# Wide first products for pairs of tiles, second products ten steps behind, some subtractions on ScalarE

## The chip, the cores and the metric

The kernel runs on one core of one Trainium2 chip. The metric is the device time of one execution in microseconds (us). Before the change it is 302.31 us, the median of three runs (301.88 to 303.08).

Five engines work side by side, each through its own queue in program order: TensorE (matmuls; PE in the profile, with weight loads listed apart as PEld), VectorE (DVE), ScalarE (ACT), GpSimd (POOL) and SyncE (SP). SP, ACT and POOL also issue DMA transfers, and an engine stands while an instruction of its queue waits.

## The reference

An attention in a sliding window, followed by a two-layer network with an ELU between. Cut to what matters:

```python
def _attn_ref(q, k, v):                      # (8, 8, 576, 64): batch, heads, sequence, head size
    scores = scale * np.matmul(q, k.transpose(0, 1, 3, 2))
    mask = np.abs(pos[:, None] - pos[None, :]) <= 32
    scores = np.where(mask, scores, -1000000000.0)
    attn = np.exp(scores - np.max(scores, axis=-1, keepdims=True))
    attn = attn / (np.sum(attn, axis=-1, keepdims=True) + 1e-09)
    return np.matmul(attn, v)

def _moe_ref(x, w_in, w_out):                # x: (4608, 512), w_in: (512, 2048), w_out: (2048, 512)
    h = x @ w_in
    g = np.where(h > 0.0, h, np.exp(np.minimum(h, 0.0)) - 1.0)
    return g @ w_out
```

## The kernel before

**The network** is done in 18 tiles of 256 tokens. A tile has 8 steps, so there are 144 steps, counted by `kk`; `order[kk]` says which tile and which part of it a step does. Step `kk` makes two groups of 128 of the 2048 hidden features. Its *products* (`mm1`, `products`, L734) are 8 matmuls: two feature groups by four parts of the 512 inputs, each 256 columns wide. They go to one bank of PSUM, `h0` or `h1` in turn. ScalarE then takes exp of the bank (`exponents`, L744), VectorE subtracts one (`subtract`, L756; in steps 1, 3 and 4 ScalarE does it, L754), and VectorE makes g = min(max(h, 0), exp(h) - 1) from the bank and that (`elu`, L767). This last operation is issued at the beginning of step `kk + 1`, and with it the bank is free for the products of step `kk + 2`. g is kept in 8 buffers.

**The sums** (`mm2`, `add`, `sums_to`, L787) multiply g by w_out: four matmuls of 512 columns a step, two for each half of the tile's tokens, added up over the tile's 8 steps in the banks `y0` and `y1`. They run two steps (`LAG`) behind the products. With a tile's last sum, ScalarE copies y0 and VectorE copies y1 out of PSUM (`rows_out`, `copy_out`), and SP stores them. From step 132 on the sums are taken from a list `todo`, three or four a step, and `last_sums` does the rest, with the very last half tile cut into 384 and 128 columns so that its last copy is small.

**The attention** works on 36 pairs of 64-row query blocks; two pairs are the 256 tokens of one tile. From pair 6 on two pairs go together and start at step `begin[i]`, 14 steps ahead of the tile's first step: scores of both at `begin` (32 small matmuls, L384), the exp of each on ScalarE at `begin` and `begin + 1` (L395), `mask` on VectorE at `begin + 1` and `begin + 2` (L404), P.V of both at the end of `begin + 2` (`pv`, 32 small matmuls, L416), `normalize` on VectorE at `begin + 3` and `begin + 4` (L425, L428), and then `x_dma` (L455): a DMA transpose on SP that puts the pair's 128 tokens into `xT`, the input of the products. `xT` has one buffer a tile, five in turn.

**Feeding the attention**, for each batch of 576 rows: q and k are loaded as fp32 on SP (`load_qk`, L132), cast in three parts each on ScalarE (`cast_qk`), written to DRAM by ScalarE's queue (`write_rows`) and read back transposed by SP (`transpose_rows`, L324). V is loaded by GpSimd's queue (`load_v`, L151). Every second query block needs V shifted by 64 rows: `rotate_v` makes that with VectorE copies (L175), `rotate_v_dma` with two DMAs on SP (L183). Batches 2 and 3 use the DMAs, batches 4 to 7 four VectorE copies each.

**What sets the order.** It is written out by hand. `at(kk, slot, ...)` notes a task for a step, and the loop at the end runs a step as: g of the step before, the tasks "dve", the products, the tasks "mid", the sums, the tasks "end". Each engine's queue holds its instructions in the order in which this loop issues them.

Of the kernel before, what the change touches and what calls it, by code (L numbers as in the profile page):

```python
# [9 lines left out]
FP32 = mybir.dt.float32  # L10
# [11 lines left out]
def kernel(  # L22
# [100 lines left out]
    def load_qk(b, which, part, engs=(nc.sync, nc.sync)):  # L123
        z, nj = part
        mj = max(nj, HJ)
        t = lpool.tile([128, 2, mj * D], FP32, tag=f"f{which}{mj}",
                       name=f"f{which}", bufs=2 if part is WHOLE else 1)
# [166 lines left out]
    def cast_qk(b, which, part, j0, n, eng, hs=slice(0, 2)):  # L294
        z, nj = part
        if (b, which, z) not in qk_b:
            qk_b[b, which, z] = lpool.tile(
                [128, max(nj, HJ), 2 * D], BF16,
                tag=f"b{which}{max(nj, HJ)}", name="qkb",
                bufs=2 if part is WHOLE else 1)  # L300
# [142 lines left out]

    def xT_of(i):
        t, z = i // 2, i % 2
        if z == 0:
            xT[t] = xpool.tile([128, 2, NDO, 128], BF16, tag="xT", name="xT")
        return xT[t][:, z, :, :]
# [173 lines left out]
    for i in range(FIRST_TWO, NPAIR):  # L622
        begin[i] = begin.get(i - i % 2, STEPS * (i // 2) - 14)
# [17 lines left out]
    at(BACK_AT, "dve", swap_back)  # L641
    starts = set(begin.values())
    starts |= {begin[i] + 1 for i in range(FIRST_TWO, NPAIR)}
    for b in range(2, B):
# [3 lines left out]
        l_qk, l_v, c0 = {2: (0, 0, 0), 3: (15, 24, 22), 4: (35, 36, 41),  # L648
# [9 lines left out]
        if b <= 3:  # L658
# [3 lines left out]
            at((21, 28)[b - 2], "mid", rotate_v_dma, b, 3 - b)  # L662
# [16 lines left out]
        for n, (which, j0) in enumerate(  # L679
                (which, j0) for which in range(2) for j0 in (0, 6, 12)):  # L680
            at(free[n], "end", cast_qk, b, which, WHOLE, j0, 6,
               nc.vector if free[n] < 26 else nc.scalar)
            if j0 == 12:
                at(free[n], "end", write_rows, b, which)
                at(free[n] + (3 if free[n] == 29 else 4), "mid",
                   transpose_rows, b, which)

    order = [(z, n + m) for n in range(0, HALF, 2) for z in range(2)  # L690
             for m in range(2)]
    order += [(z, n) for n in range(HALF, STEPS) for z in range(2)]
    order += [(t, n) for t in range(2, NT) for n in range(STEPS)]
    psH, e_t, m_t, g_t, psY = {}, {}, {}, {}, {}

    def mm1(kk):
        t, s = order[kk]
        if kk == BY_PAIRS[1]:
            return
        ks = BY_PAIRS if kk == BY_PAIRS[0] else (kk,)  # L700
        tags = ((f"h{kk % 2}", "s") if kk == NSTEP - 1 else
                ("s",) if kk == 2 else ("u",) if kk == 3 else (f"h{kk % 2}",))
# [6 lines left out]
        for p in range(len(ks)):  # L709
            for k in ks:  # L710
                for z in range(len(tags)):
                    products(k, z, p if len(ks) > 1 else None)
                if p == len(ks) - 1:
                    for z in range(len(tags)):
                        exponents(k, z)
                        if k == NSTEP - 1:
                            elu(k, z)
# [4 lines left out]
    def products(kk, z, pair):  # L722
        t, s = order[kk]
        ps = psH[kk][z]
        w = ps.shape[1]
        for j in range(w):
# [21 lines left out]

    def subtract(kk, z):
# [3 lines left out]
        if kk in (1, 3, 4):  # L753
# [5 lines left out]
    def elu(kk, z=0):  # L759
        if z == 0:  # L760
            g_t[kk] = mpool.tile([128, FG, TT], BF16, tag="g_sb", name="g_sb",
                                   bufs=8)
# [18 lines left out]
    def sums_to(n, ts, j, c=0):  # L781
        t, s = order[n]
        if (s, ts, j) == (0, 0, 0):
            tags = ("h2", "t0") if t == 1 else ("y0", "y1")
            psY[t] = [ps_tile([128, D_MODEL], FP32, g, "psY")
                      for g in tags + ("u",) * (t == NT - 1)]
        nc.tensor.matmul(  # L787
            sum_of(t, ts, c), lhsT=g_t[n][:, j, ts * 128:(ts + 1) * 128],
            rhs=w_out_sb[:, s * FG + j, cols_of(c)],
            start=(s == 0 and j == 0),  # L790
            stop=(s == STEPS - 1 and j == FG - 1))
# [13 lines left out]
    def add(n, ts, j):  # L805
        t, s = order[n]
        for c in (1, 2) if (t, ts) == (NT - 1, 1) else (0,):
            sums_to(n, ts, j, c)
        if s == STEPS - 1 and (ts, j) == (1, FG - 1):
# [3 lines left out]
    def mm2(n):  # L813
        for ts in range(2):
            for j in range(FG):
                add(n, ts, j)
# [3 lines left out]
    LAG, LATE = 2, NSTEP - 14  # L820
    todo = [(n, ts, j) for n in range(LATE, NSTEP)
            for ts in range(2) for j in range(FG)]

    def last_sums():
        rest = sorted({n for n, _, _ in todo})
        assert len(todo) == len(rest) * 2 * FG
        def some(ns, ts, c):
            for n in ns:
                for j in range(FG):
                    sums_to(n, ts, j, c)  # L830
# [58 lines left out]
```

## Time and profile before

The profile is of one execution. Its own time is 302.52 us; the span from its first to its last instruction is 300.8 us, and the granted TensorE clock in it is 0.999.

| what | value |
|---|---|
| median of three runs | 302.31 us |
| profiled execution / its span | 302.52 us / 300.8 us |
| exp of the products, L744, ScalarE, 128x512 | 143 of 599 ns |
| subtraction, L756, VectorE, 128x512 | 140 of 435 ns |
| subtraction, L754, ScalarE, 128x512 | 3 of 631 ns |
| g, L767, VectorE, 128x512 | 143 of 690 ns |
| mask, L404, VectorE | 32 of 682 ns |
| normalisation, L425 and L428, VectorE | 36 of 199 ns and 36 of 692 ns |
| copies of y, VectorE and ScalarE, 128x512 | 17 of 683 ns, 18 of 586 ns |
| V rotation, L175, VectorE | 20 of 425 ns |
| cast of a third of q or k, ScalarE | 26 of 829 ns |
| transpose of x, L455, issue to landing | 2.6 us median, 26 issues |
| load of V, L151, issue to landing | 12.6 us median |

A count and a mean come from the groups of instructions with different shapes kept apart. A group of the page reads: line, engine, operation, output and inputs with shape, count, then busy time and mean ns of one, then the idle time of the engine just before these instructions and what ended it. Matmuls overlap each other, so their durations add up to more than the time they take: their pace is read from their starts. Some matmul records are missing from the trace, which shows as a count of 7 where 8 ran.

### The profile page before, as it was taken

The page shows a single profiled execution, that of the slowest core. Times are in us where ns is not written, and L with a number is a line of the kernel's source. Part 1 is how long each engine was busy: PE and PEld are TensorE (multiplying, and loading weights), DVE is VectorE, ACT ScalarE, POOL GpSimd, SP SyncE. Part 2 cuts the span into 40 slices and gives each one's busy share as a digit, 9 for nine tenths or more (in the row PEclk, how much of TensorE's full clock was granted, in tenths as well). Part 3 has the DMA queues.
Part 4 walks back from the last instruction along what each step waited for, and adds up shares of the span by engine and source line. Part 5 has one row for each costly group of instructions (what it writes and reads, how often), then busy time and mean ns, then how long its engine had stood idle before and what let it go on. Part 6 is the DMA issues. An engine that isn't in the chain of part 4 may idle for free.

```text
span 300.8 us, 7664 instructions
## 1 busy us (share of the span) xinstructions
PE 291.8 (97%) x3066; PEld 198.6 (66%) x3118; DVE 240.9 (80%) x479; ACT 170.2 (57%) x258; POOL 52.7 (18%) x74
## 2 busy tenths in 40 slices
PE   7899999999999999999999999999999999999995
PEld 3585567677666666666666666666666666666673
DVE  7788588978787988888889789887988787877773
ACT  3783648688655567456745665467535353534342
POOL 8777203520005000410032002300000000000000
PEclk9999999999999999999999999999999999999999
DMA  9999999999957978999899989997921111111011
GB/s 190 168 200 203 185 233 349 370 179 231 241 159 199 239 116 270 244 267 135 161 256 323 172 203 252 312 153 137 268 54 72 35 72 38 70 37 70 2 70 71
DMA packets 94070, 52.68 MB, mean 175 GB/s; under 512 B 78163, under 2 KB 83795, under 8 KB 94035
## 3 DMA queue, kind: packets, MB, share of 16 engines
q1 hardware_dynamic: 47330, 35.61, 44.7%
q0 software_dynamic: 44976, 10.10, 44.2%
q10 hardware_dynamic: 1728, 6.49, 6.3%
q8 instruction: 24, 0.39, 0.6%
q14 instruction: 12, 0.09, 0.1%
HBM read 36.70 MB, written 15.34 MB: 173 GB/s over the span
## 4 chain that ended last, share of the span: by engine, by line
PE 85%; DMA 5%; issue 3%; DVE 2%; ACT 2%; POOL 2%; POOLq 0%; ACTq 0%; DVEq 0%
PE ps L734 39%; PE psY L787 38%; PE psS L416 4%; DMA out_dram<-y_sb 3%; PE psS L384 3%; DMA c<-in_k_dram 2%; ACT e_sb L744 1%; DVE g_sb L767 1%; PE ptx L335 1%; PE psXT L438 1%; POOL Vo L158 1%; DVE qkb L292 0%; ACT qkb L290 0%; PE ptx L340 0%; PE psS L364 0%
## 5 line engine op out<-in xcount | busy, mean ns | idle before, releaser
L744 ACT ACTIVATE e_sb<-ps 128x512 f32<-128x512 f32 (+1 forms) x145 | 86.3, 596 | 113.4 <-PE ps L734 106.0
L734 PE MATMUL ps<-xT,w_in_sb 128*128 128x256 bf16 (+1 forms) x1168 | 149.7, 271 | 0.1
L787 PE MATMUL psY<-w_out_sb,g_sb 128*128 128x512 bf16 (+2 forms) x541 | 139.3, 373 | 2.9 <-issue 0.3
L734 PEld LDWEIGHTS <-w_in_sb 128*128 128x128 bf16 x1168 | 110.4, 98 | 36.8 <-issue 0.8
L767 DVE SCALAR_TENSOR_TENSOR g_sb<-ps,m_sb 128x512 bf16<-128x512 f32 (+1 forms) x145 | 99.3, 686 | 13.1 <-DVE m_sb L756 0.5
L756 DVE TENSOR_SCALAR m_sb<-e_sb 128x512 bf16<-128x512 f32 (+1 forms) x142 | 61.5, 433 | 34.3 <-ACT e_sb L744 32.3
L787 PEld LDWEIGHTS <-g_sb 128*128 128x128 bf16 x592 | 55.9, 98 | 38.7
L151 POOL DMA_DIRECT2D Ve<-in_v_dram x37 | 32.5, 892 | 132.8 <-PE psS L416 79.5
L395 ACT ACTIVATE pu<-psS 128x1024 bf16<-128x1024 f32 x36 | 36.6, 1023 | 0.9 <-PE psS L384 0.8
L428 DVE TENSOR_TENSOR x_st<-psS,rc 128x512 bf16<-128x512 f32 x36 | 24.9, 692 | 1.2
L290 ACT CAST qkb<-f 128x768 bf16<-128x768 f32 (+1 forms) x29 | 25.0, 862 | 0.0
L404 DVE TENSOR_TENSOR pm<-pu,masks 128x1024 bf16<-128x1024 bf16 x32 | 21.8, 682 | 0.0
L416 PEld LDWEIGHTS <-pm 128*64 128x64 bf16 x512 | 9.6, 110 | 7.3 <-DVE pm L404 6.5
L292 DVE COPY y_sb<-psY 128x512 f32<-128x512 f32 (+1 forms) x18 | 12.2, 676 | 1.5 <-PE psY L787 1.5
L384 PEld LDWEIGHTS <-kT 64*128 64x128 bf16 x560 | 9.4, 95 | 4.6 <-issue 4.4
L290 ACT COPY y_sb<-psY 128x512 f32<-128x512 f32 (+1 forms) x19 | 10.8, 569 | 2.5 <-PE psY L787 2.5
L384 PE MATMUL psS<-qT,kT 64*128 64x64 bf16 x560 | 11.8, 191 | 0.1
L416 PE MATMUL psS<-Ve,pm 128*64 128x65 bf16 x288 | 11.5, 196 | 0.1
L290 ACT COPY qT<-ptx 128x1152 bf16<-128x1152 bf16 (+4 forms) x9 | 7.7, 882 | 5.0 <-PE ptx L340 3.5
L416 PE MATMUL psS<-Vo,pm 128*64 128x65 bf16 x224 | 10.3, 196 | 0.0
L175 DVE COPY Vo<-Ve 64x1040 bf16<-64x1040 bf16 (+1 forms) x22 | 9.1, 413 | 0.7
L425 DVE RECIPROCAL rc<-psS 128x8 f32<-128x8 f32 x36 | 7.2, 199 | 0.9 <-PE psS L416 0.9
(54 smaller groups left out, 91.3 us busy)
## 6 DMA issues: line engine op xcount, KB each, us to landing
out_dram<-y_sb SPq DMA_DIRECT2D x36, 256.0 KB, 3.5
f<-in_q_dram SPq DMA_DIRECT2D x12, 576.0 KB, 6.3
f<-in_k_dram SPq DMA_DIRECT2D x12, 576.0 KB, 8.0
in_dram<-qkb ACTq DMA_DIRECT2D x10, 576.0 KB, 4.2
Ve<-in_v_dram POOLq DMA_DIRECT2D x21, 128.0 KB, 12.6
w_out_sb<-in_moe_w_out_dram POOLq DMA_DIRECT2D x3, 512.0 KB, 10.4
Ve<-in_v_dram POOLq DMA_DIRECT2D x14, 96.0 KB, 11.6
w_in_sb<-in_moe_w_in_dram POOLq DMA_DIRECT2D x2, 512.0 KB, 10.4
```

The costliest lines, as they stand in the source:

```text
L151: nc.gpsimd.dma_start(out=V_e[b % 3][p0:p1, m, :, 0:D], in_=v[b, :, lo + p0:lo + p1, :].rearrange("h p d -> p h d"))
L290: nc.scalar.copy(d_, s_)
L384: nc.tensor.matmul(psS[:, h % 2, hp * 128 + z * QB:hp * 128 + (z + 1) * QB], lhsT=keys, rhs=qT[b % 2][base:base + 64, hp, QB * qb:QB * (qb ...
L395: nc.scalar.activation(pu, _bap(psS, [psS.ap[0], [1, 1024]]), AX.Exp, scale=SCALE)
L404: nc.vector.tensor_mul(pm, pu, _bap(mm, [mm.ap[0], [0, H], [1, 2 * QB]]))
L416: nc.tensor.matmul(psS[QB * z:QB * (z + 1), par, hp * VD:(hp + 1) * VD], lhsT=pm[:, par * HP + hp, z * QB:(z + 1) * QB], rhs=vv[:, qb // 2 ...
L428: nc.vector.tensor_mul(x_st, _bap(psS, [psS.ap[0], [VD, HP], [512, 2], [1, D]]), _bap(rc, [rc.ap[0], [2, HP], [1, 2], [0, D]]))
L734: nc.tensor.matmul(o, lhsT=w_in_sb[:, do, fo * 128:(fo + 1) * 128], rhs=r, start=(do == 0), stop=(do == NDO - 1))
L744: nc.scalar.activation(e_sb, ps, AX.Exp)
L756: nc.vector.tensor_scalar(m_sb, e_sb, -1.0, None, ALU.add)
L767: nc.vector.scalar_tensor_tensor(g_t[kk][:, z * w:(z + 1) * w, :], ps, 0.0, m_t.pop((kk, z)), ALU.max, ALU.min)
L787: nc.tensor.matmul(sum_of(t, ts, c), lhsT=g_t[n][:, j, ts * 128:(ts + 1) * 128], rhs=w_out_sb[:, s * FG + j, cols_of(c)], start=(s == 0 an ...
```

## The change

1. **Wide products.** From tile 8 on (`WIDE`), two tiles share their products. A step makes one feature group for both tiles: 4 matmuls of 512 columns, where a step made two groups for one tile with 8 matmuls of 256 columns. A pair of tiles has 16 such steps, 64 to 79 for tiles 8 and 9. `xT` becomes one buffer for the four pairs of two tiles (two in turn), and for the earlier tiles four buffers. The attention of tiles 8 to 17 begins two steps earlier.
2. **Sums from a list.** From step 18 on all sums of tiles 2 to 16 come from `todo`, in order: four a step, or three in the steps of the set `light` from step 31 (`FALL`) on, as long as fewer than 48 (`LEAD`) are owed; a tile's last sums are finished in the step when at most one more than these is left. The sums of the last tile are done after all others, in `last_sums`, in the banks h0, u and s. g has 23 buffers.
3. **Subtraction.** Besides steps 1, 3 and 4, ScalarE subtracts in steps 30 to 89 that are two to four steps after the begin of pairs 8 to 19 and have no cast: steps 30, 33, 34, 35, 39, 50, 51 and 52.
4. **Feeding.** Batch 4's V is rotated by DMAs at step 43; its casts start at step 40. The load and cast tiles of q and k are two in turn for wholes and halves alike, where halves had their own.

```diff
     def load_qk(b, which, part, engs=(nc.sync, nc.sync)):
         z, nj = part
-        mj = max(nj, HJ)
-        t = lpool.tile([128, 2, mj * D], FP32, tag=f"f{which}{mj}",
-                       name=f"f{which}", bufs=2 if part is WHOLE else 1)
+        t = lpool.tile([128, 2, SJ * D], FP32, tag=f"f{which}",
+                       name=f"f{which}")
...
     def xT_of(i):
-        t, z = i // 2, i % 2
+        n = 2 if i < 2 * WIDE else 4
+        t, z = i // n * n // 2, i % n
         if z == 0:
-            xT[t] = xpool.tile([128, 2, NDO, 128], BF16, tag="xT", name="xT")
+            xT[t] = xpool.tile([128, n, NDO, 128], BF16, tag=f"xT{n}",
+                               name="xT", bufs=4 if n == 2 else 2)
...
-        begin[i] = begin.get(i - i % 2, STEPS * (i // 2) - 14)
+        begin[i] = begin.get(i - i % 2, STEPS * (i // 2) - 14 - 2 * (i >= 2 * WIDE))
...
-        l_qk, l_v, c0 = {2: (0, 0, 0), 3: (15, 24, 22), 4: (35, 36, 41),
+        l_qk, l_v, c0 = {2: (0, 0, 0), 3: (15, 24, 22), 4: (35, 36, 40),
...
-        if b <= 3:
+        if b <= 4:
...
-            at((21, 28)[b - 2], "mid", rotate_v_dma, b, 3 - b)
+            at((21, 28, 43)[b - 2], "mid", rotate_v_dma, b, int(b == 2))
...
-    order += [(t, n) for t in range(2, NT) for n in range(STEPS)]
+    order += [(t, n) for t in range(2, WIDE) for n in range(STEPS)]
+    made = {(t, n * FG + j): (kk, j * TT)
+            for kk, (t, n) in enumerate(order) for j in range(FG)}
+    for t in range(WIDE, NT, 2):
+        for fo in range(NFO):
+            for z in range(2):
+                made[t + z, fo] = len(order), z * TT
+            order.append((t, fo))
...
+        if t >= WIDE:
+            for do in range(NDO):
+                nc.tensor.matmul(
+                    _bap(ps, [ps.ap[0], [128, 4], [1, 128]]),
+                    lhsT=w_in_sb[:, do, s * 128:(s + 1) * 128],
+                    rhs=xT[t][:, :, do, :],
+                    start=(do == 0), stop=(do == NDO - 1))
+            return
...
+    busy = {begin[i] + n for i in range(8, 20) for n in (2, 3, 4)}
+    on_scalar = {1, 3, 4} | {kk for kk in busy - casts if 30 <= kk < 90}
+
     def subtract(kk, z):
...
-        if kk in (1, 3, 4):
+        if kk in on_scalar:
             nc.scalar.activation(m_sb, e_sb, AX.Copy, bias=-1.0)
...
-    LAG, LATE = 2, NSTEP - 14
-    todo = [(n, ts, j) for n in range(LATE, NSTEP)
-            for ts in range(2) for j in range(FG)]
+    LAG, FALL, LEAD = 2, 31, 12 * 2 * FG
+    todo = [(t, n * FG + j, ts) for t in range(2, NT - 1)
+            for n in range(STEPS) for ts in range(2) for j in range(FG)]
+    ALL = (NT - 3) * NFO * 2
+    light = {begin[i] + n for i in range(FIRST_TWO, NPAIR)
+             for n in (0, 2, 5, 6, 7)} - writes
+
+    def more_sums(kk):
+        behind = (kk + 1 - 2 * STEPS) * 2 * FG - (ALL - len(todo))
+        n = 3 if FALL <= kk and kk in light and behind < LEAD else 4
+        left = len(todo) % (2 * NFO) or 2 * NFO
+        for _ in range(left if left <= n + 1 else n):
+            if not todo or made[todo[0][:2]][0] > kk - LAG:
+                break
+            add(*todo.pop(0))
...
     def last_sums():
...
+        for ts, c in ((0, 0), (1, 1), (1, 2)):
+            for fo in range(NFO):
+                sums_to(NT - 1, fo, ts, c)
+            if c == 1:
+                copy_out(NT - 1, ts, c, nc.vector)
+            else:
+                rows_out(NT - 1, ts, c, nc.scalar)
```

## The prediction

> **What bounds the kernel now.** I read the page's engine totals, slices and groups first, then the time line of all engines in one stretch of the steady part, and last the landing times of the transposes that bring x.
>
> ```profile
> PE 291.8 (97%) x3066; PEld 198.6 (66%) x3118; DVE 240.9 (80%) x479; ACT 170.2 (57%) x258; POOL 52.7 (18%) x74
> ...
> PE   7899999999999999999999999999999999999995
> ...
> L734 PE MATMUL ps<-xT,w_in_sb 128*128 128x256 bf16 (+1 forms) x1168 | 149.7, 271 | 0.1
> L787 PE MATMUL psY<-w_out_sb,g_sb 128*128 128x512 bf16 (+2 forms) x541 | 139.3, 373 | 2.9 <-issue 0.3
> L734 PEld LDWEIGHTS <-w_in_sb 128*128 128x128 bf16 x1168 | 110.4, 98 | 36.8 <-issue 0.8
> ```
>
> TensorE is full from the third slice to the last but one, and its two large groups had 0.1 and 2.9 us of idle time before them in the whole run: nothing that only feeds it sooner can gain. So I need its true pace, and how closely the engines that release its banks follow. Both are in the time line of steps 107 to 111 (start, duration, what):
>
> ```profile
> 228.75 0.60 ACT L744 ACTIVATE e_sb<-ps 128x512 f32<-128x512 f32 x1 [0.90 <-PE ps L734]
> ...
> 229.38 0.43 DVE L756 TENSOR_SCALAR m_sb<-e_sb 128x512 bf16<-128x512 f32 x1 [0.59 <-ACT e_sb L744]
> 229.42 1.04 PE L734 MATMUL ps<-xT,w_in_sb 128*128 128x256 bf16 x8
> 229.92 0.69 DVE L767 SCALAR_TENSOR_TENSOR g_sb<-ps,m_sb 128x512 bf16<-128x512 f32 x1
> ...
> 230.29 1.03 PE L787 MATMUL psY<-w_out_sb,g_sb 128*128 128x512 bf16 x4
> 230.49 0.60 ACT L744 ACTIVATE e_sb<-ps 128x512 f32<-128x512 f32 x1 [0.22 <-PE ps L734]
> 230.53 0.68 DVE L404 TENSOR_TENSOR pm<-pu,masks 128x1024 bf16<-128x1024 bf16 x1
> ...
> 231.53 0.42 PE L416 MATMUL psS<-Ve,pm 128*64 128x65 bf16 x16
> ...
> 233.64 1.04 PE L734 MATMUL ps<-xT,w_in_sb 128*128 128x256 bf16 x8
> ...
> 234.51 1.03 PE L787 MATMUL psY<-w_out_sb,g_sb 128*128 128x512 bf16 x4
> ...
> 235.37 0.82 PE L734 MATMUL ps<-xT,w_in_sb 128*128 128x256 bf16 x6
> ```
>
> Starts, not durations, give the pace. Eight products take 234.51 - 233.64 = 0.87 us, four sums 235.37 - 234.51 = 0.86. Averaged over such steps a step is 1.735, split 0.872 and 0.863: 109.0 ns for 256 columns, 215.7 for 512. Each change to the attention's small matmuls and back costs about 0.1 us.
>
> **The loop that may bind.** Products of step k fill bank h(k mod 2). Step k+2 may overwrite it after exp (0.2 after the products' end), subtract (0.63 after exp's start: 229.38 - 228.75) and the g operation (0.53 later, lasting 0.69): 2.07 us in all. TensorE fills that time with sums of k, products of k+1 and sums of k+1: 0.86 + 0.87 + 0.86 = 2.60, spare 0.53. In steps 132 to 134 of this kernel, with three sums each, the spare is 0.65 + 0.87 + 0.65 = 2.17 less 2.07, or 0.10. They keep their pace (1.52 from start to start), VectorE having nothing else to do there:
>
> ```profile
> 276.22 1.04 PE L734 MATMUL ps<-xT,w_in_sb 128*128 128x256 bf16 x8
> 277.09 0.81 PE L787 MATMUL psY<-w_out_sb,g_sb 128*128 128x512 bf16 x3
> 277.74 1.04 PE L734 MATMUL ps<-xT,w_in_sb 128*128 128x256 bf16 x8
> ```
>
> **The change part by part.** *Wide products.* Steps 64 to 143 issue 4 matmuls of 512 columns where 8 of 256 stood: 872 - 863 = 9 to 11 ns a step (the averages are read to 1 ns a matmul), times 80: 0.8 us gained. The 320 weight loads that go (320 x 98 ns = 31 us) run beside matmuls today and gain nothing. If a 512-column product cost two of 256, the gain would be 0; I take 0.8, since the sums' row has that very width.
>
> The Trainium skill, page "TensorE: Matmul & The Clock Gate", section "Back-to-back issue gap", gives about 131 ns for a 512-column matmul in a stream with weight loads; by it the 320 wide products would gain some 27 us more, an estimate. The sums are such a stream and stand at 215.7 ns here, so I give the rule no weight. The page "Perfetto Trace Analysis", section "Identifying the Most-Contended Engine", judges TensorE's headroom by the share of weight loads, 66% here, which this change lowers by ten points; the 0.1 us of idle before the products says that this share binds nothing.
>
> *Sums ten steps behind.* Their number stays. From step 31 on some steps do 3 or 2 sums (2 in steps 44, 63, 73), the others 4, until 44 to 48 are owed; these come after the last products, where TensorE needs nobody. That moves work at no cost, but it uses up the spare wherever VectorE has extra work. Step by step, in the order in which the build puts the work:
>
> - Second mask of two pairs. The g operation of the first mask's step starts 1.38 after its products' end, the mask 0.61 later, lasting 0.68: done at 2.67. TensorE reaches the second pair's P.V after sums, products, sums, 0.10 for the change of kind and 0.28 for the first pair: 2.98 with 4+4 sums (in the time line: mask done 231.21, used 231.53). With 3+3 (steps 33, 39, 50) it is 2.55: 0.12 late, three times, 0.35. With 3+2 (step 44) 2.33: 0.34 late. In step 74 (2+3, 2.33) the copy of a finished y in step 73 comes first (+0.40, as step 105 of this trace shows: bank free at 2.46): 0.75 late. Sum 1.4 us.
> - Copy of y in a step with 3 sums (53): bank free at 2.47 against 2.17, 0.3 late.
> - V rotation on VectorE, 0.46 a piece from start to start: in step 62 (3+2 sums, 1.95) free at 2.23, 0.3 late; in steps 69 and 70 (3+3) at 2.25 and 2.4 against 2.17, 0.1 + 0.2 late.
>
> The last two make 0.9, together 2.3 us of waiting. Bounds: 0 if VectorE's links run quicker than a busy queue shows, 3.2 if each of these nine places loses 0.1 more. I take 2.3. From step 80 on, with 4 sums and y's copy beside the second mask, the 0.53 covers all.
>
> *Subtraction on ScalarE* in the eight steps 30, 33 to 35, 39, 50 to 52. It takes 631 ns there (the row of L754), so the bank comes free at 2.19 instead of 2.07, but VectorE saves 0.53 each, which the list above counts (it is why step 34's copy of y costs nothing). 0.12 lies in the spare of 4-sum steps; without that cover it is 8 x 0.12 = 1 us.
>
> *x for two tiles at once.* All four pairs of tiles 8 and 9 must lie in xT at step 64. The last transpose is issued in step 60, 2.06 us after the start of that step's products (143.74 against 141.68 now). Steps 60 to 63 last 1.73 + 1.52 + 1.52 + 1.30 = 6.07, so 4.0 us remain. Now ten steps lie between. Landings of the two issued from 202.5 us on, and of the two from 159.0 us on:
>
> ```profile
> DMA to landing us min/median/max: 2.4/3.6/4.8
> ```
>
> ```profile
> DMA to landing us min/median/max: 9.2/9.2/9.3
> ```
>
> The second kind stands right behind a q and k load on SP. In the new order batch 5's load is issued in step 52, eight steps ahead, so I take 2.4 to 4.8: 0 to 0.8 late, value 0.2. Steps 80 and 96 leave 4.4 and 4.8 us.
>
> *V rotation of batch 4 by DMA* (step 43): two issues on SP, which wait for V loads of steps 36 to 40 (10 to 13 us to landing), so SP stands some 6 us. Behind them wait two stores of y, two transposes of x (needed at step 56) and the q and k transposes of batch 4 (steps 48 and 51, needed at 56, some 2 us to spare). VectorE saves 4 x 0.42. Cost 0; if that room were gone, about 1 us.
>
> *Load tiles shared* by halves and wholes: batch 3's load waits for the casts of steps 14 and 15 (48 us instead of 46), is needed at 60 us and lands in 6 to 8: nothing. *The tail*: 28 whole and 32 part sums after the last products, every g long made; the last 128-column copy and its store stay: nothing.
>
> **Sum.** The profiled execution took 302.52 us, 300.8 of them span: 302.52 - 0.8 + 2.3 + 0.2 = 304.2. That execution lies 0.2 above the median of 302.31, so I forecast 304.0.
>
> **The rivals.** *The small waits don't come*, the other side: if VectorE releases 0.15 us sooner at each place, only 0.2 + 0.6 (steps 44, 74), 0.15 + 0.15 (53, 62) and 0.05 (70) are left: 302.3 - 0.8 + 1.1 = 302.6, no change; without any wait 301.5. For it: VectorE idles 0.59 before a subtraction in the time line. Against: it is 80% busy, and a mask ends 0.3 before its use. What decides is whether the bank is free by 2.17 us beside extra work. *x lands late*: if step 60's transposes meet traffic as at 159 us, 9.3 - 4.0 = 5.3 us at step 64: 309. Against: no load stands ahead of them. *Wide products gain more*: one such matmul at 205 ns would give 320 x 10 = 3.4 us, 300.6; the sums' row speaks against it.
>
> **How the numbers follow.** Forecast 58%, small waits absent 33%, x late 6%, more gain 3%. About 0.5% (1.5 us) is what a measurement of this kernel can tell from no change: bounds 300.8 and 303.8. Of the forecast, between 303.2 and 305.5, 303.8 cuts off about a quarter: 43% slower, 15% the same. So faster 0.03, same 0.33 + 0.15 = 0.48, slower 0.43 + 0.06 = 0.49. The range, 301.4 to 306.3, takes in the bounds of the waits and part of a late landing.
>
> **What would show it.** Right: wide products whose four take 0.863 us; waits of TensorE for the g operation and the mask between 85 and 180 us, none after; none for xT. Wrong: no wait from step 31 to 80, or wide products far from 215.7 ns.

## The result: 310.5 us, 2.8% slower

| kernel | median (lowest to highest) | ratio to the kernel before, 95% interval |
|---|---|---|
| before | 302.11 us (301.83 to 303.08, 6 runs) | |
| changed | 310.54 us (309.51 to 312.10, 6 runs) | 1.0277 (1.0246 to 1.0307) |

The profiled execution of the changed kernel took 310.79 us, with a span of 309.1 us and a granted clock of 1.0. The page's engine totals, TensorE's slices and its groups, as shown of the kernel before:

```profile
PE 293.1 (95%) x2757; PEld 167.2 (54%) x2798; DVE 238.9 (77%) x465; ACT 174.9 (57%) x265; POOL 51.5 (17%) x74
...
PE   8999999999999999997978998999999999999995
...
L813 PE MATMUL psY<-w_out_sb,g_sb 128*128 128x512 bf16 (+2 forms) x552 | 140.8, 373 | 4.4 <-issue 1.9
...
L740 PE MATMUL ps<-xT,w_in_sb 128*128 128x512 bf16 x320 | 82.2, 380 | 4.4 <-DVE g_sb L792 4.1
L754 PE MATMUL ps<-xT,w_in_sb 128*128 128x256 bf16 (+1 forms) x528 | 66.7, 270 | 0.4 <-DMA w_in_sb<-in_moe_w_in_dram 0.2
```

The weight loads' share has fallen from 66% to 54%, as it must with 320 fewer. TensorE's own share has fallen too, from 97% to 95%: it waits. The dips (7, 7, 8) stand in slices 19, 21 and 22, from 139 to 147 and from 155 to 170 us, and the wide products (L740) have 4.4 us of idle time before them where the products had 0.1.

Where it waits is read from the starts of TensorE's matmuls, taking off each group's own pace, and that of a matmul whose record is missing. From step 20 on the kernel before has no such gap over 0.1 us. The changed kernel has 9.1 us of them:

| steps | gap, us | what TensorE waits for |
|---|---|---|
| 33, 39, 44, 50 | 0.17, 0.23, 0.39, 0.17 | second mask, VectorE |
| 55, 63 | 0.34, 0.22 | bank, behind a copy of y and a V copy on VectorE |
| 74 | 0.95 | copy of y0 on ScalarE |
| 31, 35 | 0.71, 0.46 | two copies on ScalarE, behind a subtraction |
| 64 | 2.05 | x of tiles 8 and 9 |
| 70, 71, 72 | 0.24, 0.85, 1.03 | bank, behind V copies on VectorE |
| 87, 88 | 0.30, 0.81 | the same |
| 79 | 0.22 | a single gap |

After step 88 there is none. There the steady pace shows the gain: the eight steps from 98 to 106 take 15.24 us, where the kernel before takes 15.32. Over 80 steps that is 0.8 us. From step 31 to the last matmul: 9.1 us of gaps less 0.8 is 8.3, and the two traces differ by 8.27 there.

**V copies.** VectorE's time line over steps 69 to 71 (start, duration, instruction), then GpSimd's:

```profile
154.47 0.43 DVE L781 TENSOR_SCALAR m_sb<-e_sb 128x512 bf16<-128x512 f32 x1
155.01 0.69 DVE L792 SCALAR_TENSOR_TENSOR g_sb<-ps,m_sb 128x512 bf16<-128x512 f32 x1
155.73 0.62 DVE L174 COPY Vo<-Ve 64x1040 bf16<-64x1040 bf16 x1
156.38 0.88 DVE L781 TENSOR_SCALAR m_sb<-e_sb 128x512 bf16<-128x512 f32 x1
157.37 0.69 DVE L792 SCALAR_TENSOR_TENSOR g_sb<-ps,m_sb 128x512 bf16<-128x512 f32 x1
158.09 0.93 DVE L174 COPY Vo<-Ve 64x1040 bf16<-64x1040 bf16 x1
159.05 0.75 DVE L781 TENSOR_SCALAR m_sb<-e_sb 128x512 bf16<-128x512 f32 x1
...
155.35 4.20 POOL L150 DMA_DIRECT2D Ve<-in_v_dram  x5 [26.85 <-PE ps L740]
```

From 60 us on the copy and the subtraction took 0.43 us at most wherever GpSimd was idle. While GpSimd issues the five V loads of the next batch, from 155.35 to 159.55, these four take 0.62 to 0.93. Not every one is stretched: a copy at 187.31, beside the next such issue, took 0.43. The g operation, which reads PSUM, keeps its 0.69. In the kernel before the same two copies stood at 160.32 and 162.03, just behind GpSimd's issue (155.61 to 159.87), and took 0.43 and 0.42.

**x.** The two last transposes of x for tiles 8 and 9, and the matmuls that need them. First the rows of the line that issues the transposes, between 133 and 146 us, then TensorE's time line:

```profile
L457 SPq DMA_TRANSPOSE xT<-x_st x2: 1189/1206/1223, 135.8 to 138.1; - x2
...
who waited for it (us, times):
  PEld L740: 2.3, 1
```

```profile
141.90 0.60 PE L813 MATMUL psY<-w_out_sb,g_sb 128*128 128x512 bf16 x2
...
144.35 0.56 PEld L740 LDWEIGHTS <-w_in_sb 128*128 128x128 bf16 x4 [2.35 <-issue]
144.38 1.02 PE L740 MATMUL ps<-xT,w_in_sb 128*128 128x512 bf16 x4 [1.88 <-DVE g_sb L792]
```

Issued at 135.8 and 138.1, they landed at 142.26 and 144.24 by their semaphore events, 6.4 and 6.2 us later. (The 144.1 that an expectation below gives for the first is the landing of another transfer, ScalarE's write of the cast q rows.) The last one is what TensorE waits for. A reader must be careful here: the bracket of the matmul names VectorE's g operation, which had ended long before the start at 144.38. The weight load ahead of it carries the wait for the transposes.

**ScalarE.** Its time line in step 30 and 31, and the second pair's scores:

```profile
78.91 0.84 ACT L289 CAST qkb<-f 128x768 bf16<-128x768 f32 x1
...
80.46 0.60 ACT L764 ACTIVATE e_sb<-ps 128x512 f32<-128x512 f32 x1 [0.71 <-DVE x_st L425]
81.09 0.63 ACT L779 ACTIVATE m_sb<-e_sb 128x512 bf16<-128x512 f32 x1
...
81.62 0.57 ACT L289 COPY xT<-psXT 128x512 bf16<-128x512 bf16 x1
...
82.24 0.41 PE L381 MATMUL psS<-qT,kT 64*128 64x64 bf16 x16 [0.54 <-ACT xT L289]
```

The moved subtraction (L779, 0.63) stands ahead of ScalarE's copy of the transposed x out of bank u, and the second pair's scores want that bank. In step 35 it stands in the same way ahead of the copy of y0.

### The profile page after: what moved, and what is told of

Same layout as the page of the kernel before. It is cut to its first block, busy times and chain, and to the rows that moved or that the text cites. A ratio compares the mean times of both kernels' runs of the same rounds, so it can differ in the third digit from the quotient of the medians.

```text
span 309.1 us, 7031 instructions
## 1 busy us (share of the span) xinstructions
PE 293.1 (95%) x2757; PEld 167.2 (54%) x2798; DVE 238.9 (77%) x465; ACT 174.9 (57%) x265; POOL 51.5 (17%) x74
## 4 chain that ended last, share of the span: by engine, by line
PE 69%; DVE 9%; DMA 9%; ACT 4%; issue 4%; POOL 3%; ACTq 1%; DVEq 0%; POOLq 0%
PE psY L813 30%; PE ps L740 19%; PE ps L754 13%; DMA w_in_sb<-in_moe_w_in_dram 6%; DVE g_sb L792 3%; PE psS L413 3%; PE psS L381 3%; ACT e_sb L764 3%; DVE m_sb L781 2%; DMA Vo<-in_v_dram 2%; PE ptx L337 1%; DVE Vo L174 1%; POOL c L144 1%; ACT qkb L289 1%; DVE y_sb L291 1%
## 5 line engine op out<-in xcount | busy, mean ns | idle before, releaser
L764 ACT ACTIVATE e_sb<-ps 128x512 f32<-128x512 f32 x144 | 86.0, 598 | 109.7 <-PE ps L740 75.1
L813 PE MATMUL psY<-w_out_sb,g_sb 128*128 128x512 bf16 (+2 forms) x552 | 140.8, 373 | 4.4 <-issue 1.9
L792 DVE SCALAR_TENSOR_TENSOR g_sb<-ps,m_sb 128x512 bf16<-128x512 f32 x144 | 99.2, 690 | 16.3 <-ACT m_sb L779 4.2
L781 DVE TENSOR_SCALAR m_sb<-e_sb 128x512 bf16<-128x512 f32 x133 | 59.5, 448 | 35.6 <-ACT e_sb L764 34.3
L740 PE MATMUL ps<-xT,w_in_sb 128*128 128x512 bf16 x320 | 82.2, 380 | 4.4 <-DVE g_sb L792 4.1
L754 PE MATMUL ps<-xT,w_in_sb 128*128 128x256 bf16 (+1 forms) x528 | 66.7, 270 | 0.4 <-DMA w_in_sb<-in_moe_w_in_dram 0.2
L754 PEld LDWEIGHTS <-w_in_sb 128*128 128x128 bf16 x528 | 48.5, 98 | 15.5 <-issue 0.7
L150 POOL DMA_DIRECT2D Ve<-in_v_dram x37 | 31.4, 866 | 135.1 <-DVE Ve L169 42.7
L740 PEld LDWEIGHTS <-w_in_sb 128*128 128x128 bf16 x320 | 30.5, 97 | 41.9 <-issue 6.5
L413 PE MATMUL psS<-Ve,pm 128*64 128x65 bf16 x288 | 12.3, 197 | 0.1
```

The lines of the kernel that those rows point to most:

```text
L150: nc.gpsimd.dma_start(out=V_e[b % 3][p0:p1, m, :, 0:D], in_=v[b, :, lo + p0:lo + p1, :].rearrange("h p d -> p h d"))
L413: nc.tensor.matmul(psS[QB * z:QB * (z + 1), par, hp * VD:(hp + 1) * VD], lhsT=pm[:, par * HP + hp, z * QB:(z + 1) * QB], rhs=vv[:, qb // 2 ...
L740: nc.tensor.matmul(_bap(ps, [ps.ap[0], [128, 4], [1, 128]]), lhsT=w_in_sb[:, do, s * 128:(s + 1) * 128], rhs=xT[t][:, :, do, :], start=(do ...
L754: nc.tensor.matmul(o, lhsT=w_in_sb[:, do, fo * 128:(fo + 1) * 128], rhs=r, start=(do == 0), stop=(do == NDO - 1))
L764: nc.scalar.activation(e_sb, ps, AX.Exp)
L781: nc.vector.tensor_scalar(m_sb, e_sb, -1.0, None, ALU.add)
```

## The experiments

Each ratio is to the kernel before, run on the same chip in the same session (medians 302.05 to 302.41 us).

### What stretches VectorE's copies

Three kernels: V copies moved away from GpSimd's issue, GpSimd's issue moved away from the copies, and GpSimd's issue moved onto the copies in the kernel before.

```diff
-            for n, back in enumerate((10, 8, 3, 2)):
+            for n, back in enumerate((10, 8, 0, 0)):
```

> The changed kernel with the second pair of V copies on VectorE of batches 5 to 7 moved from 3 and 2 steps ahead of the batch's first scores to the scores' own step; no transfer is touched. In the changed kernel those of batch 6 and 7 stand in the 4.2 us in which GpSimd issues V loads, and TensorE waits 2.1 us in steps 70 to 72 and 1.1 us in steps 87 and 88. Theory (VectorE's copies and subtractions are stretched from 0.43 to 0.6 to 0.9 us by GpSimd's issue, and the copies are what brings them into the way): most of these 3.2 us go, 307 to 308.5 us. Rival (the waits come from the sums given up there, not from the place of the copies): the waits stay in size and move by two steps, 310 to 311 us.

310.23 us, 1.0265 (1.0234 to 1.0297): the same as the changed kernel. But the waits went as the theory has it: steps 70 to 72 kept 0.46 of 2.12 us, steps 87 and 88 nothing of 1.11. There were new ones, 2.17, 0.45 and 0.55 us in steps 61, 62 and 66: the cast of q in step 58 stood 3.60 us for its load (next part). Step 64 had 0.51 here. These are not the edit's doing: nothing that it moves runs before step 69. Ahead of the products of step 64, this kernel, the changed one, the one with earlier V loads (next) and the one with narrow products (below) issue the same work and the same transfers in the same order, and yet steps 61 to 64 wait 3.1, 2.3, 0.7 and 0.9 us in their profiled executions. So the cause was right, and the time did not show it; and a gap in these steps, from one profiled execution, is no measure of an edit.

```diff
-                         5: (52, 52, 57), 6: (68, 68, 73),
-                         7: (84, 84, 89)}[b]
+                         5: (52, 52, 57), 6: (68, 65, 73),
+                         7: (84, 81, 89)}[b]
```

> The loads of V of batches 6 and 7 go from steps 68 and 84 to steps 65 and 81, so that GpSimd is done issuing them when VectorE makes the V rotations of steps 69, 70, 85 and 86. Theory (while GpSimd issues these loads, VectorE's copies and subtractions between SBUF tiles take 0.74 to 0.93 us instead of 0.43, and the banks of steps 69 to 71 and 85 to 87 come free late): rotations and subtractions of 0.43 us there, the waits of 2.1 us at steps 69 to 71 and of 1.1 us at 86 and 87 fall to 0.3 and 0, so 3 us less than the changed kernel, 307.5. Rival (VectorE is simply too full in shortened steps): durations don't matter, at most 0.5 us less, 310.

313.85 us, 1.0350 (1.0287 to 1.0414). Steps 70 to 72 fell to 0.62, and 87 and 88 lost their wait for VectorE. In step 88 a new one stood: 3.2 us for the transposed k of the next batch, whose DMA now shared its time with V.

```diff
 (kernel before)
-                         5: (52, 52, 57), 6: (68, 68, 73),
+                         5: (52, 52, 57), 6: (68, 70, 73),
```

> The kernel before, with one number changed: the V loads of batch 6 are issued from step 70 on instead of 68, so that GpSimd's issue meets the V copies of steps 71 and 72. Theory (the stretching is one of the chip and has nothing to do with wide products or late sums): the two copies and the subtractions beside them take 0.6 to 0.9 us instead of 0.43, and TensorE, which waits nowhere after step 20 of the kernel before, waits 0.3 to 1.5 us in steps 72 to 74; 302.6 to 304 us. Rival (the stretching belongs to the changed kernel alone): they stay at 0.43, 302 us.

303.24 us, 1.0028 (1.0014 to 1.0042). VectorE's time line in this kernel, and the wait of TensorE that follows:

```profile
159.22 0.43 DVE L756 TENSOR_SCALAR m_sb<-e_sb 128x512 bf16<-128x512 f32 x1
...
160.47 0.62 DVE L175 COPY Vo<-Ve 64x1040 bf16<-64x1040 bf16 x1
161.12 0.88 DVE L756 TENSOR_SCALAR m_sb<-e_sb 128x512 bf16<-128x512 f32 x1
...
162.83 0.42 DVE L175 COPY Vo<-Ve 64x1040 bf16<-64x1040 bf16 x1
163.29 0.68 DVE L756 TENSOR_SCALAR m_sb<-e_sb 128x512 bf16<-128x512 f32 x1
...
160.09 4.43 POOL L151 DMA_DIRECT2D Ve<-in_v_dram  x5 [30.97 <-PE ps L734]
```

```profile
162.85 1.03 PE L734 MATMUL ps<-xT,w_in_sb 128*128 128x256 bf16 x8 [0.46 <-DVE g_sb L767]
```

The copy and the subtraction beside GpSimd's issue take the same 0.62 and 0.88 us as in the changed kernel, with narrow products and sums in step. The other copy, at 162.83, stands beside the issue too and kept 0.42; no run shows why. TensorE loses 0.6 us at once and 0.8 in all. The stretching comes without any part of the change.

### What makes x, q and k late

In the changed kernel x stands ahead of the q and k loads on SP; before, it stood behind them. The V loads of batch 5 run at the same time on GpSimd's queue.

```diff
-                         5: (52, 52, 57), 6: (68, 68, 73),
+                         5: (52, 48, 57), 6: (68, 68, 73),
```

> The loads of V of batch 5 go from step 52 to step 48. Theory (the two last transposes of x for tiles 8 and 9, issued at 135.8 and 138.1 us, landed at 144.1 and 144.2 because V's small packets of these loads fill the DMA engines until about 140 us): they land within 5 us of their issue, step 64 waits 0.5 us or less instead of 2.05, 1.5 to 2 us less than the changed kernel, 308.8. Rival (the write of the cast q rows, issued at 138.5 us, is what the transposes stand beside): they land as late as now and the time stays at 310.5.

316.40 us, 1.0453 (1.0421 to 1.0484). The scores of step 56 waited 3.1 us for k, whose transpose now ran beside V. And step 64 kept its wait, 2.1 us: all of V had landed by 130.8, and still the two last transposes, issued at 141.0 and 143.3, took 5.9 and 6.2 us. The q and k loads, now later, landed up to 144.3, two stores of y up to 145.8, and the write of the cast q rows, issued at 143.65, at 149.3. So x is late without V beside it as well; V is at most a part of the cause.

```diff
-                         5: (52, 52, 57), 6: (68, 68, 73),
+                         5: (52, 60, 57), 6: (68, 68, 73),
...
-            for n, back in enumerate((10, 8, 3, 2)):
+            for n, back in enumerate((6, 4, 0, 0) if b == 5 else (10, 8, 0, 0)):
```

> The kernel with late V copies, and the V loads of batch 5 issued from step 60 on, behind the transposes of x for tiles 8 and 9, instead of from step 52 on (their copies follow at 6 and 4 steps and 0 steps ahead of the scores). Theory (those transposes land 6 to 8 us after issue since they share the queues with batch 5's loads): they land within 5 us, the 2.1 us of waiting in step 64 falls under 0.5, and the time lies 1 to 2 us under that of the kernel with late V copies. Rival (they are late for another reason, the q and k loads or the queue's own order): step 64 still waits 1.5 us or more, same time as with late copies.

310.45 us, 1.0268 (1.0249 to 1.0288): no gain. The rows of the line that issues x's transposes:

```profile
who waited for it (us, times):
  PE ps L740: 0.5, 1
...
DMA to landing us min/median/max: 2.5/2.5/2.5
```

This view knows the landing of the first of the two alone. It took 2.5 us, as fast as any in these traces, where the kernel with late copies and V loads from step 52 took 7.2. The last, issued at 138.33, landed at 143.14 by its semaphore events, 4.8 us later (4.4 with late copies), and the products of step 64 start at 143.28: step 64 still waits 0.70 for x, as the row above says. Beside this last transpose stand the write of the cast q rows (138.70 to 142.76) and V in its new place, issued from 139.0 to 143.4 us. The waits of steps 61 and 62 are down to 0.21. What is won there is lost later: the cast of batch 6's q in step 74 stands 3.04 us for its load, and steps 77 and 78 wait 1.75 us.

```diff
-            at(l_qk, "end", load_qk, b, 0, WHOLE)
-            at(l_qk, "end", load_qk, b, 1, WHOLE)
+            at(l_qk, "mid" if b > 4 else "end", load_qk, b, 0, WHOLE)
+            at(l_qk, "mid" if b > 4 else "end", load_qk, b, 1, WHOLE)
...  (and l_qk of batches 5, 6, 7 is 51, 67, 83 instead of 52, 68, 84)
```

> The changed kernel with the q and k loads of batches 5, 6 and 7 put back ahead of the two transposes of x on SP, where the kernel before has them: there SP issues the loads of batch 5 at 123.4 us right behind a transpose of k and x after them; in the changed kernel x, two steps earlier, stands ahead of the loads and these follow at 126.6 us. Theory (the loads, 3.2 us later on busy queues, make the x transposes of tiles 8 and 9 late, and ScalarE's cast of the loaded q too): the transposes of 135.8 us land within 5 us, step 64 waits under 0.5 us instead of 2.05, the cast waits for nothing, 308 to 309 us. Rival (x is late since two tiles are wanted at once, whatever stands ahead): step 64 still waits 1.5 us or more, 310 us.

312.12 us, 1.0314 (1.0282 to 1.0347). The two last transposes land 5.4 and 3.8 us after their issue, step 64 waits 0.15, and no cast waits. But TensorE waits 2.3 us in step 61, 0.45 in step 62 and 0.91 in step 66. VectorE's time line in steps 59 and 60 shows why:

```profile
134.61 0.20 DVE L422 RECIPROCAL rc<-psS 128x8 f32<-128x8 f32 x1
137.94 0.69 DVE L425 TENSOR_TENSOR x_st<-psS,rc 128x512 bf16<-128x512 f32 x1 [3.14 <-DMA xT<-x_st]
138.55 0.42 DVE L781 TENSOR_SCALAR m_sb<-e_sb 128x512 bf16<-128x512 f32 x1
```

The normalisation writes into a buffer that an earlier transpose of x, now behind the loads, has not yet read; subtraction and g stand behind it. The rival fell too, but the order on SP alone is not the cause: the lateness moved from q and the last x to the x before.

With late V copies as well, that is, this edit and `(10, 8, 0, 0)` together:

> The same with the second pair of V copies on VectorE moved from 3 and 2 steps ahead of the scores to the scores' step, which by themselves took away 2.7 us of waits, but met a wait of 2.6 us in steps 61 and 62 behind a cast that waited 3.6 us for the load of q. Theory (that wait comes from the late load): it is gone, and both gains add up: waits of TensorE of some 4 us in all instead of 9.3, 305 to 306.5 us. Rival (a wait of 2 us comes back at some other place between steps 55 and 66): 308 us or more.

310.47 us, 1.0286 (1.0216 to 1.0356), from 308.88 to 312.86. The profiled run, the fastest, has 7.4 us of gaps, 2.1 of them in steps 61, 62 and 64 and 1.1 in step 96. The rival came true.

The same order, put into the kernel before:

```diff
 (kernel before)
-                         5: (52, 52, 57), 6: (68, 68, 73),
+                         5: (54, 52, 57), 6: (68, 68, 73),
```

> The kernel before with the q and k loads of batch 5 put behind the two transposes of x on SP (step 54 instead of 52), as the changed kernel has them. Theory (the order on SP makes loads and x late in any kernel; the kernel before has more room, since tile 8 alone must lie there in step 64 and the casts start later): ScalarE's cast in step 57 waits 1 to 4 us for the load and TensorE waits up to 3 us near steps 58 to 60; x of tile 9, needed in step 72, is in time; 302.5 to 305 us. Rival (the old kernel has room for it): 302 us, no wait of TensorE over 0.3 us.

306.43 us, 1.0122 (1.0085 to 1.0159). ScalarE and then TensorE:

```profile
132.84 0.58 ACT L290 COPY y_sb<-psY 128x512 f32<-128x512 f32 x1
137.36 0.83 ACT L290 CAST qkb<-f 128x768 bf16<-128x768 f32 x1 [3.94 <-DMA f<-in_q_dram]
138.10 0.59 ACT L744 ACTIVATE e_sb<-ps 128x512 f32<-128x512 f32 x1
```

```profile
136.51 0.81 PE L787 MATMUL psY<-w_out_sb,g_sb 128*128 128x512 bf16 x3
140.00 1.03 PE L734 MATMUL ps<-xT,w_in_sb 128*128 128x256 bf16 x8 [2.67 <-DVE g_sb L767]
```

The load was issued 6.4 us later (129.78 instead of 123.41). The cast, first in ScalarE's queue, waits 3.9 us for it, and the exp that TensorE needs stands behind the cast. Two steps of room on SP were all that the kernel before had. The place of the wait and its size are as expected; the time lies above the 305 us expected, since TensorE ran at a lower pace after the wait (last section).

### Subtraction, width, and where sums are given up

```diff
-    on_scalar = {1, 3, 4} | {kk for kk in busy - casts if 30 <= kk < 90}
+    on_scalar = {1, 3, 4}
```

> ScalarE subtracts in steps 1, 3 and 4 only, VectorE everywhere else. Theory (the subtraction that ScalarE took over in step 30 holds up its copy of a transposed x, whose bank the scores of step 31 need, and the one in step 34 its copy of y, whose bank the sums of step 35 need): the waits of 0.7 us in step 31 and 0.46 us in step 35 go; VectorE's copy of y and normalisations then make step 36 or 37 wait some 0.5 us; net 0.3 to 0.9 us less than the changed kernel, 310. Rival (VectorE needs this help): steps 33 to 53 wait more, 1 us or more above the changed kernel, 311.5.

309.60 us, 1.0244 (1.0229 to 1.0260). The gaps of steps 31 and 35 are gone, 1.17 us; steps 36 and 37 have new ones of 0.56, and step 39 has 0.52 instead of 0.23. That is 0.3 us better, beside which step 64 had 0.77 in this run. The move to ScalarE cost a little more than it gained.

```diff
-            for do in range(NDO):
-                nc.tensor.matmul(
-                    _bap(ps, [ps.ap[0], [128, 4], [1, 128]]),
-                    lhsT=w_in_sb[:, do, s * 128:(s + 1) * 128],
-                    rhs=xT[t][:, :, do, :],
+            for z in range(2):
+                for do in range(NDO):
+                    nc.tensor.matmul(
+                        ps[:, z, :],
+                        lhsT=w_in_sb[:, do, s * 128:(s + 1) * 128],
+                        rhs=xT[t][:, 2 * z:2 * z + 2, do, :],
```

> From tile 8 on each product of 512 columns is made as two of 256, with a weight load each, 320 matmuls and 320 weight loads more; everything else as in the changed kernel. Theory (a 512-column product costs 215.7 ns, two of 256 cost 218): a plain step goes from 1.725 to 1.735 us, 0.8 us more in all, 311.3, and the waits stay where they are. Rival (weight loads count): several us more.

311.00 us, 1.0316 (1.0254 to 1.0379); the interval holds that of the changed kernel, so the time alone settles nothing. The pace does: steps 98 to 106 take 15.32 us, as in the kernel before, against 15.24 with wide products. In these two traces the gap of step 64 was 0.69 here and 2.05 there.

With late copies, the subtraction on VectorE, and the sums given up by a list of steps (none done in steps 31, 37, 48 and 64; one to three in sixteen others; 56 sums are owed in the end, not 48):

```diff
-        n = 3 if FALL <= kk and kk in light and behind < LEAD else 4
+        n = SUMS.get(kk, 4)
```

> The kernel with late V copies, the subtraction on VectorE again from step 30 on, and the 48 sums given up by a list of steps chosen so that few of them stand beside masks, copies of y or V copies (all four of them in most steps with scores). Theory (the waits of steps 31, 33, 35, 39, 44, 50, 53, 62 and 74 come from sums given up where VectorE or ScalarE has extra work): these 3.5 us fall to about 1, what is left is the wait for x in step 64 (0.4 to 2.1 in the kernels so far): 303.5 to 306 us. Rival (sums ten steps late cost by themselves, whatever the step they are taken from): 307 us or more.

311.93 us, 1.0329 (1.0292 to 1.0367). A miss: 9.6 us of gaps. 2.9 of them stand in step 64; but the masks and copies did not fall to 1 us either, since y's copies now met others, and the steps next to those without sums had nothing to cover their waits (0.44 in step 32, 1.2 in steps 70 to 72).

With late copies, loads ahead of x, and three sums given up with the scores:

```diff
         n = 3 if FALL <= kk and kk in light and behind < LEAD else 4
+        if n == 3 and kk in begin.values():
+            n = 1
```

> The same again, and three sums instead of one given up in the steps with scores, so that fewer are given up beside masks and copies of y. Theory (a sum given up costs only where VectorE or ScalarE has extra work, and beside scores TensorE has 0.68 us of other work): waits of masks and of step 74 shrink, 304 to 305.5 us. Rival (what is given up in one place is missed in the next): same as the kernel without this edit within 0.5 us, or slower.

308.76 us, 1.0212 (1.0176 to 1.0248), the fastest form of the changed kernel that ran. The gaps of steps 35, 55 and 74 are gone, 1.75 us; steps 46 to 57 have new ones of 1.05, and step 64 waits 1.79.

### The shift alone

```diff
 (kernel before)
-        begin[i] = begin.get(i - i % 2, STEPS * (i // 2) - 14)
+        begin[i] = begin.get(i - i % 2, STEPS * (i // 2) - 14 - 2 * (i >= 16))
...
-        l_qk, l_v, c0 = {2: (0, 0, 0), 3: (15, 24, 22), 4: (35, 36, 41),
+        l_qk, l_v, c0 = {2: (0, 0, 0), 3: (15, 24, 22), 4: (35, 36, 40),
```

> The kernel before with one part of the change alone: the scores of tile 8's pairs and of all later ones two steps earlier (and the first cast of batch 4 one step earlier, as the changed kernel has it, so that the order on SP is the same), but narrow products for one tile, four sums a step and the subtraction on VectorE as they were. Theory (the DMA and GpSimd part of the loss, 2.1 us in step 64 and 3.2 us in steps 69 to 72 and 87, 88, comes from this shift against loads that stay at their steps): VectorE's V copies of steps 69 and 70 take 0.6 to 0.9 us beside GpSimd's issue and TensorE waits 0.5 to 1.5 us after each such pair; loads that follow x on SP make a cast of steps 58 to 63 wait, for 1 to 3 us of TensorE; no wait at masks. 304 to 307 us. Rival (these losses need the steps shortened by given-up sums): 302 to 303 us.

311.14 us, 1.0286 (1.0234 to 1.0338): the whole loss, without wide products, late sums or subtraction on ScalarE. But it is not the same loss. The part with V copies is: steps 71, 72, 87 and 88 wait 0.62, 0.80, 0.28 and 0.80 us. The part with loads did not come: no cast waits, and x, needed for one tile at a time, is in time. The largest part nobody had named. ScalarE in step 49:

```profile
118.27 0.60 ACT L744 ACTIVATE e_sb<-ps 128x512 f32<-128x512 f32 x1 [0.90 <-PE ps L734]
118.77 1.02 ACT L395 ACTIVATE pu<-psS 128x1024 bf16<-128x1024 f32 x1
119.67 0.59 ACT L290 COPY y_sb<-psY 128x512 f32<-128x512 f32 x1
```

```profile
PE psY L787 <- ACT y_sb L290: 3.4, 10, 0.3
```

Two steps earlier, the second pair's exp (L395) falls into the step in which a tile's sums end, the copy of y0 stands behind it, and the sums of the next tile start 0.5 us late, in each of ten tiles: 5.05 us by the starts (the view counts less, since it takes a matmul's time to its modelled end). In the changed kernel the sums are ten steps late, y ends in another step, and this wait is not there after step 74. The lateness of the sums thus seems to pay for itself; that rests on the comparison of these two kernels, which differ in more than the sums.

### Putting the repairs together

The kernel with three sums given up beside scores, with batch 5's V behind x:

```diff
-                         5: (51, 52, 57), 6: (67, 68, 73),
+                         5: (51, 60, 57), 6: (67, 68, 73),
...
-            for n, back in enumerate((10, 8, 0, 0)):
+            for n, back in enumerate((6, 4, 0, 0) if b == 5 else (10, 8, 0, 0)):
```

> The kernel with the loads ahead of x, late V copies and three sums given up beside scores, and the V loads of batch 5 from step 60 on, behind x, instead of from 52 on. Theory (its 0.8 us in step 62 and 1.8 us in step 64 come from batch 5's V loads, which share the DMA engines with q, k and x from 123 to 140 us): both fall under 0.5 in all, and 305.5 to 307 us remain of 308.8. Rival (q, k, the write of rows and x are enough to make each other late): step 64 still waits over 1 us, 308 us or more.

317.38 us, 1.0446 (1.0356 to 1.0537). Steps 62 and 64 fell to 0.21 and 0.35, as expected; the first of the two last transposes landed in 2.5 us, the last in 4.8. Then the scores of step 72 waited 7.6 us for k:

```profile
PE psS L381 <- DMA kT<-in_dram: 7.6, 1, 7.6
```

```diff
-    on_scalar = {1, 3, 4} | {kk for kk in busy - casts if 30 <= kk < 90}
+    on_scalar = {1, 3, 4} | {kk for kk in busy - casts if 31 <= kk < 90}
```

> The same, with the subtraction of step 30 back on VectorE. Theory (that subtraction delays ScalarE's copy of the transposed x and so the second pair's scores in step 31 by 0.71 us): that wait goes, 0.5 to 0.8 us less than the kernel without this edit, 305 to 306 us; still not below the kernel before, since the gain of the wide products, 0.8 us, is all that stands on the other side. Rival (below before): under 302 us.

The wait of step 31 is gone, and step 32 waits 0.23. The k of step 72 is as late as before (8.1 us in the profiled run). Its four runs lie at 310.5 and at 315.3 to 317.5 us, too far apart for a ratio. No form of the changed kernel that ran comes near the kernel before.

## Why the prediction was wrong

- **Direction: right. Time: wrong**, 304.0 against 310.5, above the range's 306.3. **Mechanism: right for 2.5 of the 9.1 us of waiting**, the small waits; right in place but far too cheap for the V copies; wrong for the subtraction on ScalarE and for x. Of the signs that it named, waits for g and masks came, and none after step 88; "none for xT" failed.
- **Wide products, 0.8 us:** right, by the pace of the tile with and without them. The rival that they gain more is out.
- **Small waits of masks, copies of y and the V copy of step 62:** 2.0 us predicted, 2.5 measured (0.96 + 0.34 + 0.22 + 0.95). Right in place; only in step 74 it was ScalarE's copy of y0, and not the mask, that ended last. The rival without these waits is out.
- **V copies of steps 69 and 70, 0.3 us; 2.1 measured, and 1.1 more in steps 87 and 88**, where the prediction let a spare of 0.53 cover all. The failed step is the price "0.46 a piece from start to start". It came from copies beside an idle GpSimd. The trace of before held the warning: a subtraction of 0.56 us at 156.96, while GpSimd issued. It was a faint one: of nine subtractions that ran beside such an issue from 60 us on, two were stretched (0.50 and 0.56); what decides it is not shown. The Trainium skill, page "SBUF — State Buffer", section "Who interferes with whom", says that VectorE and GpSimd share a port pair, that copies and `tensor_scalar` can take it, and that whoever comes second waits for the other's whole instruction. Which operations stretch agrees (copy and subtraction, not g); the size here is a stretch from 0.43 to 0.62 to 0.93 us, less than one of GpSimd's five issues takes (0.78 to 0.91), and some copies and subtractions beside an issue keep 0.43.
- **Subtraction on ScalarE, 0; 1.2 measured in steps 31 and 35.** The prediction counted when the bank of the products comes free. It did not name what is queued behind the subtraction on ScalarE: two copies that free other banks. With the subtraction back on VectorE these waits went and 0.85 us came elsewhere, so the net loss was 0.3.
- **x for two tiles, 0.2; 2.05 measured** in the profiled run, 0.15 to 2.9 in the others with V loads from step 52. The failed step is "no load stands ahead of them", with the landing of 2.4 to 4.8 us that it allowed: the last transpose took 6.2. The q and k loads stand eight steps ahead in SP's order, as the prediction says, but SP issued them at 126.6 to 128.5 us, in steps 55 and 56, and by their semaphore events they landed up to 138.4 us, two stores of y behind them up to 140.1, and batch 5's V, issued on GpSimd's queue from 124.3 us on, up to 142.3, all after the first transpose of x was issued at 135.8. Which of these transfers makes x late is not shown. With V behind x (three kernels) the first of the two transposes landed in 2.5 us, with V from step 52 (nine kernels) in 4.9 to 7.2; but the last one, which decides, took 4.8 to 5.0 there and 3.8 to 7.3 in the nine, and 6.2 with V from step 48. ScalarE's write of the cast q rows is on its way beside the last transpose in every one of these kernels, and no run takes it from there: this rival stays open. The rival "x lands late" had the mechanism and a price of 5.3.
- **V of batch 4 by DMA, the load tiles, the tail:** no wait stands at them.

The common root: the scores move two steps, and with them x, casts, V copies and writes, while the loads keep their steps. The prediction checked each moved instruction against its own queue, and not against what runs at that time on other engines.

What stays open: why x lands at such different times in the same order (step 64 waited from 0.5 to 2.1 us in kernels that issue the same up to there), and whether some placement of batch 5's q, k, V and x lets all be in time.

## What to carry to other kernels

Moving a stage in an order written by hand moves it past everything that stays: list what every other engine and the DMA engines do in the new step, not only the moved instruction's own queue. A duration holds for the neighbours it was measured beside; before using a VectorE copy's row, look for one beside a GpSimd that issues DMAs. Where DMA engines are full, as here from 130 to 138 us, moving one load only chose which of its rivals was late.

## What the hardware showed unasked

A long wait of TensorE can cost more than itself. In the kernel before with loads behind x, TensorE stood for 2.8 us. Windows of 4 us around it (busy time of each engine, then granted clock, DMA share, GB/s):

```profile
134.00:138.00 4.00, 3.27 (x48) 2.07 (x49) 0.60 (x1) 0.64 (x1) 0.00 (x0) 1.00 0.99 398
138.00:142.00 4.00, 2.00 (x11) 1.19 (x11) 3.07 (x6) 3.93 (x7) 0.00 (x0) 0.86 0.58 227
142.00:146.00 4.00, 3.95 (x48) 2.53 (x48) 2.49 (x6) 1.32 (x3) 0.00 (x0) 0.71 0.10 20
```

After the wait the granted clock falls to 0.71 in the next window, and the first sums, by their starts, come 0.43 us apart instead of 0.216. After the wait of 2.2 us in step 61 of the kernel with late copies it stayed at 1.00 from 136 to 146 us; after one of 2.1 us in step 64 of the kernel with V loads from step 48 it fell to 0.62 (150 to 153 us). So the length of the wait alone does not decide it.
